# Two value tiles written to memory and read back row by row through indexed transfers

## The chip, the cores and the metric

The kernel runs on one core of a Trainium2 chip. The core has TensorE (PE in the profile; PEld is its weight load), VectorE (DVE), ScalarE (ACT), GpSimd (POOL) and SyncE (SP), which issues most of the transfers. Each engine works through its own list of instructions in order and waits on semaphores for the others. Transfers run on 16 DMA engines; SP and POOL each issue theirs on a queue of their own. The metric is the device time of one execution in microseconds (us), lower is better.

## The reference, cut to what matters

```python
# q, k, v: (4, 8, 768, 64); centroids: (8, 16, 64); w_in: (512, 2048); w_out: (2048, 512)
q_assign = argmax(q_n @ c_n.T); k_assign = argmax(k_n @ c_n.T)      # per head, 16 clusters
scores = q @ k.T / 8, masked to q_assign == k_assign
attn   = softmax(scores);  x = attn @ v                             # (4, 8, 768, 64)
x      = x.transpose(0, 2, 1, 3).reshape(3072, 512)
h = x @ w_in;  g = h - tanh(h);  out = g @ w_out                    # (3072, 512)
```

So there are 4 batches of 8 heads with 768 tokens each, an attention in which a token sees only the tokens of its own cluster, and a two-layer block on the result.

## The kernel before, in words

**Pairs and steps.** The eight heads of a batch are taken two at a time. A pair is `n` = 0 to 15: pairs 0 to 3 are the first batch, pairs 12 to 15 the fourth. The queries of a pair are cut into two halves of 384, its keys into six blocks of 128. A step is (pair, half, two key blocks), so a pair has six steps and there are 96 in all. In the late batches the steps follow each other pair by pair.

**What a step does.** One loop over the steps (`for at, (n, half, s) in enumerate(steps)`, L1223) writes the order of every engine by hand:

- `begin` (L491) issues the next step's scores on PE (`sc`, L499) and their exponential on ACT (L521).
- `value` (L549) multiplies the weights `e` by the values: `av` on PE, L556. It reads `vals[n][:, h, j]`, the 128 x 64 block of head `h` and key block `j`, and a step takes two of the six blocks, in order.
- `select` (L523) masks the next step's exponentials on DVE (`e`, L531), and after the second of a step's two tiles POOL adds the weights up into `sum` (L543 for the first step of a half, L547 twice for the others). The weights live in a pool of two buffers, so the mask of a step needs POOL's sum of the step two before to be done.
- After both halves of a pair, `total_both` (L610) adds `sum` over the partitions with four small matmuls on PE (`den`, L617). They wait for POOL's last addition to `sum`.

**What is put between.** While a batch's pairs run, the two-layer block of the batch before is put between the steps' matmuls (`fills`, L1214). From the first step of pair 12 it is the third batch's: first eight rounds `i` of seven products on PE (`pu`, L933), whose results DVE adds into `G` (L928); ACT takes the tanh of each round's two parts (`th`, L1000, a pool of two buffers), POOL subtracts it (`G`, L1002) and makes two further combinations per round (L1007, L1008). Then come 21 products `pd` (L1029) that read all of `G`. The first of them needs every round's first part.

**The queue of small jobs.** What else a step has to do is collected in the list `todo` (L1302), which is dealt out evenly between the products of the step (`between`, L1358). `turn`, `route_on` and `publish` of the next pair, the check of the weights' range (L1156) and the like are in it.

**The values.** A pair's values are loaded by SP with two transfers (L333, 192 KB each, one per head) into one of two buffers of `vals`, at the end of the pair two before. The load of pair 13 is issued by SP at 576.12 us, that of pair 14 at 632.22 us, that of pair 15 at 689.74 us. Nothing else touches `vals` before `value` reads it.

**POOL's transfers before.** POOL issues 32 loads of raw weights (L218) and 30 stores of results (L755, L1048); each moves 128 rows. The instruction waits for the transfer that used the same one of eight semaphores before it.

Of the kernel before, what the change touches and what calls it, by code (L numbers as in the profile page):

```python
# [30 lines left out]
F32 = mybir.dt.float32  # L31
BF16 = mybir.dt.bfloat16
I32 = mybir.dt.int32
# [6 lines left out]
P = 128  # L40
# [18 lines left out]
def kernel(  # L59
# [10 lines left out]
    nc = tc.nc  # L70
# [3 lines left out]
    B, H, S, D = q.shape  # L74
# [3 lines left out]
    NCH = S // P  # L78
    HP = H // 2
# [13 lines left out]
    const = ctx.enter_context(tc.tile_pool(name="const", bufs=1))  # L93
    dram = ctx.enter_context(tc.tile_pool(name="dram", bufs=6, space=DRAM))
# [84 lines left out]
    def fast():  # L179
# [48 lines left out]
            fetch(at + AHEAD)  # L228

        def constants():  # L230
            nc.vector.memset(inverses, 0.0)
            make_identity(nc, ident)
            nc.vector.memset(ones, 1.0 / words)
            nc.vector.memset(wholes, 0.0)

            mine_first = const.tile([P, 1], F32, name="mine_first")
            nc.vector.tensor_reduce(
                out=mine_first, in_=ident.rearrange("p (a b) -> p a b", b=D // 2)[:, :, 0], axis=AX.X,
                op=ALU.add,
            )  # L240
            nc.vector.tensor_copy(out=firsts, in_=mine_first.to_broadcast([P, D]))
            for c in range(C):
                nc.vector.memset(down[:, c : c + 1], float(C - c))

            spread_ = const.tile([P, 2, D], F32, name="spread_")
            nc.vector.memset(spread_, 0.0)
            nc.vector.tensor_copy(
                out=spread_[:, :, 0:C], in_=down.unsqueeze(1).to_broadcast([P, 2, C])
            )
            spread_ = spread_.rearrange("p a c -> p (a c)")  # L250
            nc.vector.tensor_tensor(out=spread_, in0=spread_, in1=ident, op=ALU.mult)
            nc.vector.reduce_sum(out=mine_code, in_=spread_, axis=AX.X)
# [54 lines left out]
        raw_qk, vals, turned, codes, q_codes = {}, {}, {}, {}, {}  # L307
# [5 lines left out]
        def rowwise(n: int):  # L313

            return n < HP

        def load(n: int, what=(0, 1)):
            if n >= len(pairs):
                return
            b, p = pairs[n]  # L320
            for i in what:
                if i < 2:
                    pool, tag = (gp, "g") if b == 0 else (loads, f"x{i}")
                    shape = [P, NCH, 2, D] if rowwise(n) else [P, NBL, BL]
                    t = raw_qk[n, i] = pool.tile(shape, F32, name=f"x{i}", tag=tag)
                else:
                    pool = vp0 if n in (2, 3) else vp
                    t = vals[n] = pool.tile([P, 2, NCH, D], F32, name="vals")
                for h in range(2):
                    src = (q, k, v)[i][b, 2 * p + h]  # L330
                    if i == 2 or rowwise(n):
                        order = "(p j) d -> p j d" if i and rowwise(n) else "(j p) d -> p j d"
                        nc.sync.dma_start(  # L333
                            t[:, :, h] if i < 2 else t[:, h], src.rearrange(order, p=P)
                        )
                        continue
                    blocks = src.rearrange("(b t) d -> t b d", t=BL)
                    for w in range(D // BL):
                        r = h * D + w * BL
                        nc.sync.dma_start(t[r : r + BL], blocks[:, :, w * BL : (w + 1) * BL])  # L340

        def turn(n: int, i: int, engine):

            if not rowwise(n):
                x = raw_qk.pop((n, i))
                pool = turnp0 if n in (2, 3) else turnp
                t = turned[n, i] = pool.tile([P, 2, TB], F32, name=f"t{i}")
                nc.vector.transpose(  # L348
                    out=t.rearrange("p a n -> p (a n)"), in_=x.rearrange("p b d -> p (b d)")
                )  # L350
                return
            pt = ps_s.tile([P, 2, 512], F32, name="pt", tag="s")
            x = raw_qk.pop((n, i))
            for j in range(NCH):
                nc.tensor.transpose(
                    out=pt[:, j // HCH, (j % HCH) * P : (j % HCH + 1) * P],
                    in_=x[:, j].rearrange("p h d -> p (h d)"), identity=ident,
                )
            pool = turnp0 if n in (2, 3) else turnp
            t = turned[n, i] = pool.tile([P, 2, TB], F32, name=f"t{i}")  # L360
            if engine is nc.scalar:
                nc.scalar.copy(out=t, in_=pt[:, :, 0:TB])
            else:
                nc.vector.tensor_copy(out=t, in_=pt[:, :, 0:TB])
# [75 lines left out]
        rows, hots = {}, {}  # L440
# [551 lines left out]
        def strassen_items(b: int):  # L992
# [82 lines left out]
        steps = [(p, half, s) for half in range(2) for p in range(HP) for s in range(NS)] + [  # L1075
            (n, half, s) for n in range(HP, len(pairs)) for half in range(2) for s in range(NS)
        ]
# [20 lines left out]


        ready = {}  # L1100
        TURN_Q, LOAD = 6, 7
        for n in range(2, len(pairs)):
            if n < HP:
                first_step, places = 3 * (n - 2), (0, 1, 1, 2, 2, 4)
            else:
                first_step = steps.index((n - 1, 0, 0) if n > HP else (n - 2, 1, 0))
                places = (-1, 0, 1, 3)
            for i, stage in enumerate(before(n)):
                if stage:
                    ready.setdefault(first_step + places[i], {})[i] = stage  # L1110
            if n >= HP:
                ready.setdefault(first_step + 1, {})[LOAD] = lambda n=n: load(n + 1)
                if not rowwise(n):
                    ready[first_step - 1][TURN_Q] = lambda n=n: turn(n, 0, nc.vector)
                ready[first_step + 1][2] = [
                    lambda n=n: similar(n), lambda n=n: turn_back(n), lambda n=n: route(n),
                    lambda n=n: route_on(n),
                ]
# [43 lines left out]
        rounding = list(range(len(PIECES)))  # L1162
        centroid_load()
        load(0)
        constants()
        keep_warm(7)
        centroid_norms()
# [3 lines left out]
        for i in range(AHEAD):  # L1171
            fetch(i)
        load(1)
        load(0, (2,))
        turn(0, 0, nc.scalar)
# [47 lines left out]
        for at, (n, half, s) in enumerate(steps):  # L1223
# [78 lines left out]
            todo = []  # L1302
# [4 lines left out]
                    todo.insert(len(todo) - 1, lambda n=n: total_both(n))  # L1307
            if LOAD in stages:
                stages[LOAD]()
            if TURN_Q in stages:  # L1310
                todo += [stages[0], stages[TURN_Q]]
            todo += [stages[i] for i in (5, 3, 4) if i in stages]
# [37 lines left out]
            if 2 * HALF <= at < 3 * HALF:  # L1350
# [3 lines left out]
                todo = todo[masks:]  # L1354
# [204 lines left out]
    with ExitStack() as cx, tc.manual_schedule():  # L1559
        fast()  # L1560
# [35 lines left out]
```

## Time and profile before

| | us |
|---|---|
| median of 2 runs (from, to) | 957.68 (957.45, 957.92) |
| the profiled execution, own time | 958.52 |
| its span in the profile | 956.7 |
| PE busy | 941.8 (98%) |
| DVE busy | 571.2 (60%) |
| POOL busy | 512.1 (54%) |
| ACT busy | 292.6 (31%) |

The clock granted to TensorE is 1.0 over the whole execution. The median, the profiled time and the span lie within 2 us of each other. "Busy" of POOL includes its arithmetic; the profile's page does not count the instructions that only issue transfers. A line of a timeline gives start, duration, engine, line of the kernel, operation, output and inputs with their shapes, how many equal instructions were merged, and in square brackets how long the engine had been idle before it and whom it waited for.

### The profile page before, as it was taken

To read this page: it belongs to the slowest core of one execution; us is meant where nothing else is said; L and a number is where in the kernel's file an instruction comes from. 1 tells how busy PE (TensorE), PEld (TensorE's weight loads), DVE (VectorE), ACT (ScalarE), POOL (GpSimd) and SP (SyncE) were. 2 spreads that over 40 slices of the span, in tenths; PEclk is the share of its full clock that TensorE was granted. 3 is DMA by queue.
4 is the path that set the end of the run, shared out by engine and by line. 5 is a ranking of instruction groups with operands and counts; after the bars stand their busy time and mean duration, and the time that the engine had idled before them with its cause. 6 is when DMAs were issued, how large, how long until landed. Compare 5 with 4: busy or idle time off the path is not lost.

```text
span 956.7 us, 16942 instructions
## 1 busy us (share of the span) xinstructions
PE 941.8 (98%) x6584; PEld 458.6 (48%) x6584; DVE 571.2 (60%) x1098; ACT 292.6 (31%) x453; POOL 512.1 (54%) x364
## 2 busy tenths in 40 slices
PE   8999999999999999999999999999999999999997
PEld 5433443345653333444455554444455555445664
DVE  7657676976776677666845567766754346443011
ACT  5575554223332332323321212333331220222000
POOL 1026353456775464777684453867796353657500
PEclk9999999999999999999999999999999999999999
DMA  7766455992736645474574746457334223323321
GB/s 196 200 188 147 141 153 128 261 258 88 196 117 157 158 143 122 151 175 130 189 191 148 181 146 184 111 179 173 110 125 146 98 81 103 116 78 132 107 106 36
DMA packets 166764, 139.85 MB, mean 146 GB/s; under 512 B 116580, under 2 KB 145044, under 8 KB 163988
## 3 DMA queue, kind: packets, MB, share of 16 engines
q1 hardware_dynamic: 160292, 117.15, 44.4%
q0 software_dynamic: 6240, 21.50, 6.8%
q8 instruction: 54, 0.88, 0.4%
q14 instruction: 34, 0.28, 0.1%
q10 hardware_dynamic: 144, 0.03, 0.0%
HBM read 117.48 MB, written 21.17 MB: 145 GB/s over the span
## 4 chain that ended last, share of the span: by engine, by line
PE 92%; DVE 2%; DMA 1%; ACT 1%; issue 1%; SPq 0%; DVEq 0%; ACTq 0%
PE pu L933 26%; PE pd L1029 23%; PE sc L499 14%; PE av L556 13%; PE o L746 8%; PE h L730 4%; PE sim L376 1%; DMA stream<-up_factors 1%; PE den L571 1%; PE den L617 1%; DVE e L531 1%; PE den L590 1%; DVE diff L899 0%; PE pq L432 0%; DVE t L348 0%
## 5 line engine op out<-in xcount | busy, mean ns | idle before, releaser
L547 POOL TENSOR_TENSOR sum<-sum,e 128x768 f32<-128x768 f32 x112 | 207.4, 1852 | 94.4 <-DVE e L531 90.2
L531 DVE SCALAR_TENSOR_TENSOR e<-row,code,sc 128x384 f32<-128x384 bf16 x336 | 185.9, 608 | 67.3 <-ACT sc L521 59.7
L521 ACT ACTIVATE sc<-sc 128x768 f32<-128x768 f32 x168 | 125.9, 789 | 229.5 <-PE sc L499 211.8
L1029 PE MATMUL pd<-stream,G 128*64 128x256 f32 x1728 | 191.2, 379 | 0.0
L933 PE MATMUL pu<-xT,stream 128*64 128x384 f32 (+1 forms) x1024 | 159.0, 447 | 1.7 <-DMA stream<-up_factors 1.1
L1029 PEld LDWEIGHTS pd<-stream,G 128*64 128x64 f32 x1728 | 123.9, 137 | 66.9 <-issue 7.2
L499 PE MATMUL sc<-t,t 64*128 64x384 f32 x768 | 150.2, 509 | 0.4 <-ACT e L521 0.3
L556 PE MATMUL av<-e,vals 128*64 128x384 f32 x768 | 145.9, 499 | 1.3 <-DVE e L531 1.3
L1002 POOL TENSOR_TENSOR G<-G,th 128x768 f32<-128x768 f32 (+1 forms) x51 | 87.1, 1724 | 69.4 <-ACT th L1000 69.2
L933 PE MATMUL pu<-diff,stream 128*64 128x384 f32 (+1 forms) x768 | 121.1, 448 | 2.8 <-DVE G L928 1.8
L933 PEld LDWEIGHTS pu<-xT,stream 128*64 128x64 f32 x1024 | 73.1, 137 | 75.8 <-issue 61.4
L499 PEld LDWEIGHTS sc<-t,t 64*128 64x128 f32 x768 | 65.9, 186 | 73.8 <-issue 37.6
L556 PEld LDWEIGHTS av<-e,vals 128*64 128x64 f32 x768 | 46.9, 136 | 86.3 <-issue 82.0
L1000 ACT ACTIVATE th<-G 128x768 f32<-128x768 f32 (+1 forms) x51 | 40.9, 806 | 148.9 <-DVE G L928 144.2
L543 POOL TENSOR_TENSOR sum<-e 128x768 f32<-128x768 f32 x28 | 52.6, 1879 | 62.8 <-DVE e L531 42.2
L746 PE MATMUL o<-w_out,g 128*64 128x512 f32 x384 | 86.1, 593 | 0.0
L933 PEld LDWEIGHTS pu<-diff,stream 128*64 128x64 f32 x768 | 53.8, 137 | 59.3 <-issue 45.2
L928 DVE TENSOR_TENSOR G<-pu,u 128x384 f32<-128x384 f32 x72 | 39.7, 552 | 32.9 <-PE pu L933 32.9
L1040 DVE SCALAR_TENSOR_TENSOR c<-pd,du 128x256 f32<-128x256 f32 x36 | 15.2, 421 | 67.1 <-PE pd L1029 67.1
L746 PEld LDWEIGHTS o<-w_out,g 128*64 128x64 f32 x384 | 27.4, 137 | 50.1 <-issue 50.0
L1040 DVE SCALAR_TENSOR_TENSOR du<-pd,du 128x256 f32<-128x256 f32 x27 | 11.4, 420 | 60.8 <-PE pd L1029 60.8
L730 PE MATMUL h<-xT,w_in 128*64 128x384 f32 x256 | 42.8, 486 | 0.0
(137 smaller groups left out, 827.0 us busy)
## 6 DMA issues: line engine op xcount, KB each, us to landing
stream<-up_factors SPq DMA_DIRECT2D x32, 896.0 KB
stream<-down_factors SPq DMA_DIRECT2D x21, 1024.0 KB
raw<-in_moe_w_in_dram POOLq DMA_DIRECT2D x16, 512.0 KB, 5.0
raw<-in_moe_w_out_dram POOLq DMA_DIRECT2D x16, 512.0 KB, 4.7
again<-in_moe_w_in_dram SPq DMA_DIRECT2D x32, 256.0 KB
again<-in_moe_w_out_dram SPq DMA_DIRECT2D x32, 256.0 KB
vals<-in_v_dram SPq DMA_DIRECT2D x32, 192.0 KB
row<-q_codes SPq DMA_DIRECT2D x29, 192.0 KB
```

The costliest lines, as they stand in the source:

```text
L499: nc.tensor.matmul(sc[i][:, h, 0:TB], lhsT=turned[n, 1][r].rearrange("p a n -> p (a n)")[:, j * P : (j + 1) * P], rhs=turned[n, 0][r, half ...
L521: nc.scalar.activation(out=out, in_=sc[i][:, :, 0:TB], func=ACT.Exp, scale=SCALE)
L531: nc.vector.scalar_tensor_tensor(out=e[:, h].rearrange("p (j n) -> p j n", n=P), in0=rows[n, half][:, h], scalar=(codes[n][:, h, 1, j : j ...
L543: nc.gpsimd.tensor_tensor(out=s, in0=pair[0], in1=pair[1], op=ALU.add)
L547: nc.gpsimd.tensor_tensor(out=s, in0=s, in1=pair[i], op=ALU.add)
L556: nc.tensor.matmul(avs[n, half][h * D : h * D + D], lhsT=vals[n][:, h, j], rhs=e[i][:, h], start=(j == 0), stop=(j == NCH - 1),)
L730: nc.tensor.matmul(h[r], lhsT=w_in[i][:, c, o * P : (o + 1) * P][:, r], rhs=xT[c][:, half], start=(c == 0), stop=(c == CD - 1),)
L746: nc.tensor.matmul(acc[sub][r], lhsT=gs[f % HF][:, f // HF, sub * P : (sub + 1) * P][:, r], rhs=w_out[f // FQ][:, f % FQ], start=(f == seq ...
L933: nc.tensor.matmul(ps[r], lhsT=streams[base + i][:, c, k_, r], rhs=right[c], start=(c == 0), stop=(c == CH - 1),)
L1000: nc.scalar.activation(out=th, in_=t, func=ACT.Tanh)
L1002: nc.gpsimd.tensor_tensor(out=t, in0=t, in1=th, op=ALU.subtract)
L1029: nc.tensor.matmul(ps[r], lhsT=left(i)[:, r], rhs=t[:, i], start=(i == 0), stop=(i == HF - 1))
```

## The change

Pairs 13 and 14 (`BY_ROWS`) get a detour for their values. When a pair's values have been loaded, twelve transfers per pair (six key blocks, two heads), issued by POOL, write them to a tile in memory of 768 rows of 64 numbers per head; twelve more read them back to the same place. Each of these 48 transfers has 128 rows of 256 B, and its rows' places in memory come from a column of indices on the chip, `places_of[:, j]`, which holds `j * 128 + p` for partition `p`: plain order. What is read back is what was written, to where it was.

The jobs are appended to `todo` in the steps of the pair before: with `at` the first step of pair `n - 1`, key blocks 0 to 2 are written in step `at + 1` and 3 to 5 in `at + 2`; blocks 0 to 2 are read back in `at + 3` and 3 to 5 in `at + 4`. A read waits for all six writes of its head. The index tile is made once at the start by POOL, ahead of the identity matrix.

```diff
         def constants():
+            nc.gpsimd.iota(places_of, pattern=[[P, NCH]], base=0, channel_multiplier=1, ...)
...
+        BY_ROWS = (3 * HP + 1, 3 * HP + 2)
+        places_of = const.tile([P, NCH], I32, name="places_of")
+        row_stores, row_moves = {}, {}
+
+        def rows_out(n: int, j: int):
+            for h in range(2):
+                if (n, h) not in row_stores:
+                    row_stores[n, h] = dram.tile([S, D], F32, name=f"rows_out{h}", bufs=len(BY_ROWS))
+                moved = nc.gpsimd.indirect_dma_start(
+                    row_stores[n, h], bass.IndirectOffsetOnAxis(ap=places_of[:, j : j + 1], axis=0),
+                    vals[n][:, h, j], None,
+                )
...
+        def rows_back(n: int, j: int):
+            for h in range(2):
+                moved = nc.gpsimd.indirect_dma_start(
+                    vals[n][:, h, j], None, row_stores[n, h],
+                    bass.IndirectOffsetOnAxis(ap=places_of[:, j : j + 1], axis=0),
+                )
+                for other_ in row_moves[n, h]:
+                    tc.add_manual_dep(moved.ins, other_.ins.name, ...)
...
+        moves = {}
+        for n in BY_ROWS:
+            for j in range(NCH):
+                at = steps.index((n - 1, 0, 0))
+                moves.setdefault(at + 1 + j // 3, []).append(lambda n=n, j=j: rows_out(n, j))
+                moves.setdefault(at + 3 + j // 3, []).append(lambda n=n, j=j: rows_back(n, j))
...
             if LOAD in stages:
                 stages[LOAD]()
+            todo += moves.pop(at, [])
             if TURN_Q in stages:
```

On POOL's list the 48 transfers fall into the stretch from 603 to 694 us of the profile before. With `W` for a write and `R` for a read, and lines of the kernel before for what stood there already, POOL's new order is:

```
pair 13: 6 W | L1002 x2, L1007, L1008, L543 | 6 W | L1002 x2, L1007, L1008, L547 x2 | 6 R | L1002,
         L547 x2 | 2 R | L1002 | 4 R | L1007, L1008, L543, L1002 x2, L1007, L1008, L547 x4, L1002
pair 14: 6 W | L1002, L1007, L1008, L543 | 6 W | L1002 x2, L1007, L1008, L547 x2 | 6 R | L547 x2,
         L1002 | 4 R | L1002 | 2 R | L1007, L1008, L1002, L543
```

On PE, DVE and SP no instruction is added; in the steps that got new jobs a few small ones (the transpose L432 and the copy L434 of the codes, the group L386 to L414, the mask L531, a check L1156, the store L438) move by about one product. `av` of pairs 13 and 14 (L556) now also waits for the reads.

More of the change, by code (lines that the diff above doesn't have):

```diff
@@ L230, in constants @@
         def constants():
+            nc.gpsimd.iota(
+                places_of, pattern=[[P, NCH]], base=0, channel_multiplier=1,
+                allow_small_or_imprecise_dtypes=True,
+            )
             nc.vector.memset(inverses, 0.0)
@@ L340, in load @@
                         nc.sync.dma_start(t[r : r + BL], blocks[:, :, w * BL : (w + 1) * BL])
+        BY_ROWS = (3 * HP + 1, 3 * HP + 2)
[9 more added lines that the diff above has]
+                )
+                for other_ in row_moves.setdefault((n, h), []):
+                    tc.declare_no_dep(moved.ins, other_.ins, reason="rows of one permutation")
+                row_moves[n, h].append(moved)
+        def rows_back(n: int, j: int):
[3 more added lines that the diff above has]
+                    bass.IndirectOffsetOnAxis(ap=places_of[:, j : j + 1], axis=0),
+                )
+                for other_ in row_moves[n, h]:
+                    tc.add_manual_dep(
+                        moved.ins, other_.ins.name,
+                        mybir.DependencyInfo(mybir.DependencyClass.Sync, mybir.DependencyReason.DATA),
+                    )
         def turn(n: int, i: int, engine):
```

## The prediction

> **What bounds the kernel now.** I read the busy times first, then the slices, then the stretch that the change touches.
>
> ```profile
> span 956.7 us, 16942 instructions
> ...
> PE 941.8 (98%) x6584; PEld 458.6 (48%) x6584; DVE 571.2 (60%) x1098; ACT 292.6 (31%) x453; POOL 512.1 (54%) x364
> ...
> POOL 1026353456775464777684453867796353657500
> ```
>
> PE is busy for 98% of the span, so nothing that PE loses can be made good later, and an instruction on another engine costs time only when PE ends up waiting for it. POOL's 54% is a mean: its slices 26 to 29 read 8, 6, 7, 7 and 9, 6 follow. The change puts all its instructions on POOL just there, so I asked for the busy times by stage:
>
> ```profile
> 603.00:700.00 97.00, 96.78 (x592) 40.73 (x590) 65.21 (x129) 34.21 (x51) 70.71 (x46) 1.00 0.51 150
> 700.00:800.00 100.00, 100.00 (x819) 57.48 (x817) 45.85 (x89) 19.95 (x31) 60.53 (x42) 1.00 0.32 107
> ```
>
> The columns are the stretch, its length, then busy time (and instructions) of PE, PEld, DVE, ACT, POOL, then clock, share of the DMA engines and GB/s. In the 97 us that take the 48 new transfers, POOL is busy for 70.7 and free for 26, and PE is full. The hundred microseconds after it are full on PE as well (100.00 of 100.00), so a delay of PE here goes to the end of the kernel undiminished. The DMA engines have half their time left.
>
> Where POOL's free time lies is shown by its timeline (rows left out in between are those where it ran on without a pause):
>
> ```profile
> 599.03 3.71 POOL L547 TENSOR_TENSOR sum<-sum,e 128x768 f32<-128x768 f32 x2 [5.68 <-DVE e L531]
> 604.58 3.60 POOL L1002 TENSOR_TENSOR G<-G,th 128x768 f32<-128x768 f32 x2 [1.84 <-ACT th L1000]
> ...
> 627.69 1.83 POOL L1002 TENSOR_TENSOR G<-G,th 128x768 f32<-128x768 f32 x1 [6.07 <-ACT th L1000]
> 629.48 3.70 POOL L547 TENSOR_TENSOR sum<-sum,e 128x768 f32<-128x768 f32 x2
> ...
> 641.26 3.60 POOL L1002 TENSOR_TENSOR G<-G,th 128x768 f32<-128x768 f32 x2 [2.36 <-ACT th L1000]
> ...
> 653.68 3.73 POOL L547 TENSOR_TENSOR sum<-sum,e 128x768 f32<-128x768 f32 x2 [3.00 <-DVE e L531]
> ...
> 665.95 1.82 POOL L543 TENSOR_TENSOR sum<-e 128x768 f32<-128x768 f32 x1 [2.84 <-DVE e L531]
> 668.59 3.59 POOL L1002 TENSOR_TENSOR G<-G,th 128x768 f32<-128x768 f32 x2 [0.82 <-ACT th L1000]
> ...
> 684.07 1.82 POOL L1002 TENSOR_TENSOR G<-G,th 128x768 f32<-128x768 f32 x1 [6.07 <-ACT th L1000]
> 685.85 4.23 POOL L547 TENSOR_TENSOR sum<-sum,e 128x768 f32<-128x768 f32 x2
> ...
> 693.97 1.00 POOL L1002 TENSOR_TENSOR G<-G,th 128x384 f32<-128x384 f32 x1
> ```
>
> The pauses from 602.74 (599.03 + 3.71) to 693.97 are 1.84 + 6.07 + 2.36 + 3.00 + 2.84 + 0.82 + 6.07 = 23.0 us. That is all that POOL has to give.
>
> Who notices when POOL is late? The chain of waits has these two among its rows (start, duration, what):
>
> ```profile
> 634.76 0.78 PE den L617 x8
> ...
> 689.85 1.12 PE den L617 x7
> ```
>
> `den` adds up POOL's `sum` at the end of pairs 12 and 13. PE takes its list in order, so at these two places it stands until POOL's L547 is done. The first comes 1.5 us after POOL's addition ends (629.48 + 3.70 = 633.18; PE's own row starts at 634.69); at the second the addition ends at 685.85 + 4.23 = 690.08 while `den` is already running: no reserve.
>
> **The change part by part.** *Removed*: nothing. *Added*: 48 transfers of 128 rows on POOL's list. The trace has no indexed transfer; its nearest rows are POOL's plain stores of 128 rows:
>
> ```profile
> L1048 POOL DMA_DIRECT2D out_dram<-c x24: 539/557/565, 495.7 to 806.3; - x24
> ...
> DMA to landing us min/median/max: 2.0/3.2/6.3
> ```
>
> The numbers are ns of one issue (least, median, most) and the time until the data has landed. Call the issue time of one indexed transfer x. From below, x is 0.56 us: as many rows, and nothing left out. From above I take 2.0 us, the shortest landing, as if the instruction held POOL until the data were there. Within that I take 1.30 us: an address per row must be formed from an index where a plain transfer steps on by a constant, so I count the 0.56 us twice (1.12), and add 0.18 us, the row of POOL's 128x1 copy into `gate` (L1170), for reading the column of indices. This is an estimate, and the whole answer hangs on it.
>
> Two rules of the Trainium skill pull it to opposite sides. "DMA: Bandwidth & Descriptors", section "Anatomy of one DMA — SWDGE (gpsimd) path", holds the making of descriptors to be small and says many can be made before it shows; by it x would stay near the plain row and the change would be free. "GPSIMD Engine Reference", section 7, prices small reads such as one per gather index at about 102 cycles each without overlap; at its 1.2 GHz, 128 of them would be about 10.9 us per transfer, an estimate from that page that would make the sum nearly 500 us. No row of this trace shows either.
>
> Now the sum, along POOL's new order.
>
> 1. *Up to the first `den`*: 12 writes and 6 reads stand ahead of L547 at 629.48. POOL falls behind by 18x; the pauses 1.84 and 6.07 and the 1.5 us of reserve are taken off. PE waits 18 × 1.30 − 9.4 = 14.0 us. On the way the tanh (L1000, two buffers) starts to wait for L1002 at about 627 (12 × 1.30 − 1.84 = 13.8 us late; 612.22 + 1.79 + 13.8 = 627.8 against 626.77), which is the same delay seen earlier, not another.
> 2. *From there to the second `den`*: POOL starts 1.5 us behind PE; 6 reads, 12 writes, 6 reads come, 24x = 31.2; the pauses 2.36, 3.00, 2.84, 0.82 and 6.07 (15.1) are taken off, and 1.8 for one L1002 that now stands behind the addition. PE waits 1.5 + 31.2 − 15.1 − 1.8 = 15.8 us.
> 3. *From there to the first `pd`*: 6 reads and that L1002 stand ahead of the L1002 at 693.97, 6x + 1.8 = 9.6. That row ends at 694.97; the first `pd` needs the last round's part only with its 15th of 16 matmuls, 14 × 0.216 us after its start at 699.04, so at 702: 7.0 us of reserve. PE waits 2.6 us.
>
> Together 14.0 + 15.8 + 2.6 = 32.4 us, or 48x − 30 wherever all three are positive. If x is 0.56, the first gives 0.7 and the others nothing.
>
> *The added waits.* The first write of a pair waits for the load of its values: SP issues pair 13's at 576.12 and pair 14's at 632.22, POOL comes to the writes at 602.7 and later than 660.9. The first read of a head waits for six writes, the last of which was issued before L1002 twice, L1007, L1008 and L547 twice: 3.6 + 1.0 + 1.0 + 3.7 = 9.3 us, against 6.3 us for the slowest landing. Were that cover gone, POOL would stand for the rest of a landing, with its sums queued behind. `av` waits for the reads: the last four of pair 13 are issued 6 × 1.30 + 1.8 = 9.6 us after the first `den`'s addition and land by 16 us, and PE needs them at 659.84, 26.7 us after it. For the others the margin is 6 us or more. All of it is free. *Memory traffic* is 48 × 32 KB twice over, 3 MB in some 90 us, with half the DMA time free: nothing.
>
> *Moved*: the small jobs on PE, DVE and SP go back or forth by about one product (1.29 us). The store of the codes (L438) goes behind one stream load; its reader L454 feeds a mask more than a step later, so the step covers it; without cover it would cost that 1.3 us, twice. *The index tile*: POOL makes it ahead of the identity. By the rows for the identity (0.20 and 0.29 us) it takes about 0.3 us; DVE first reads the identity at 1.67 us, it is ready at 1.31. Free, or some 0.3 us where not.
>
> Added to the profiled time, 958.5 + 32.4 = 990.9; the median stands 0.8 us lower, so I say 990.
>
> **The rivals.** *Cheap rows* (the other side): an indexed issue costs hardly more than a plain one, POOL's pauses swallow it, and the end stays. For it speaks that the plain rows need only 4 ns per row (0.53 to 0.57 us whether rows are 4 KB or 1 KB). Against it: POOL must fetch 128 indices first. Below x = 0.64 the sum is nothing; within 2% (19.2 us) it stays up to x = 1.02. At 0.56 it gives 958.4, at 0.8 about 966.
>
> *Dear rows*: x above 2 us, because the indices are read one at a time. At 2.5 us the sum is 48 × 2.5 − 30 = 90, that is 1048. Against it: POOL's arithmetic takes 128x768 numbers in 1.8 us, so 128 of something should not take longer unless each is fetched alone.
>
> *The transfers, not POOL*: reads land late and PE waits in `av` rather than in `den`. If every landing took the longest 6.3 us, the margins above still hold; with cheap rows the fourth read of pair 14 is issued 2 × 0.56 + 3.7 = 4.8 us before the addition for `den` ends and needed at 696.41, 6.3 us after it, so a landing of 15 us would cost PE 3.9 us, 962. *Not what it says*: the rows come back unchanged in any case; if they did not move at all it would be 957.7, and the order of instructions speaks against it.
>
> **How the numbers follow.** A measurement of this kernel tells about 2% from no change. Forecast (x from 1.02 to 2.0): 0.55. Cheap rows, with the small rivals: 0.35, of which 0.02 for a gain over 2%, since nothing is removed. Dear rows: 0.10. The range takes both bounds of x, 0.56 us (959) and 2.0 us (48 × 2.0 − 30 = 66, 1024), and leaves out the dear rows. Faster 0.02, same 0.33, slower 0.65.
>
> **What would show it.** Right: POOL's slices from 603 to 720 near 9, 48 issue rows on POOL of about 1.3 us, waits of `den` L617 and tanh L1000 for POOL of some 14 and 16 us, pauses of POOL gone, PE's products later by 32 us and otherwise equal. Step 1 is wrong if PE waits in `av` or in the mask (`e` L531) rather than at the first `den`. The forecast falls if the issue rows are under 1 us (cheap) or above 2 us (dear), or if VectorE and POOL slow each other down in the crowded stretch, which I have not priced.

## The result, and the profile after

| us | before | after |
|---|---|---|
| median (from, to), 2 runs each | 957.68 (957.45, 957.92) | 989.37 (988.44, 990.29) |
| the profiled execution, own time | 958.52 | 990.29 |
| its span | 956.7 | 988.4 |
| PE busy | 941.8 | 947.0 |
| POOL busy | 512.1 | 557.9 |

The ratio is 1.0331, 95% interval 1.0286 to 1.0375: slower by 31.7 us. In two later series, on two different chips, the changed kernel stood at 987.85 (985.82 to 988.73) and 986.90 us (986.26 to 988.23), ratios 1.0309 (1.0292 to 1.0326) and 1.0311 (1.0294 to 1.0328), which is some 30 us. Line numbers from here on are those of the changed kernel: the writes are L355, the reads L366, `den` L651, `sum` L577 and L581, `pu` L967, `pd` L1063, the tanh L1034, and POOL's combinations of `G` L1036, L1041 and L1042.

First the page of the changed kernel: span, busy times, and the slices of PE, POOL and the granted clock.

```profile
span 988.4 us, 17008 instructions
...
PE 947.0 (96%) x6584; PEld 459.6 (46%) x6584; DVE 569.9 (58%) x1098; ACT 292.7 (30%) x453; POOL 557.9 (56%) x413
...
PE   8999999999999999999999999779689999999997
...
POOL 1025443557655657677964356899899445466600
PEclk9999999999999999999999999979989999999999
```

POOL gained 45.8 us of work and its mean moved by two points of per cent. The slices tell more: slices 26 to 31 of POOL, counted from 1 and 24.7 us long each, read 8, 9, 9, 8, 9, 9, and it is there that PE falls to 7, 7, 9, 6 and 8. PE's number of matmuls is unchanged. Two slices of the clock read 7 and 8 where before there was nothing but 9.

The rows of the new instructions (duration in ns, least, median, most; then how long POOL paused before them, and the time to landing):

```profile
L355 POOL DMA_INDIRECT rows_out<-vals,places_of x24: 963/968/1049, 604.6 to 697.3; - x24
...
  issue: 6.6, 23
...
DMA to landing us min/median/max: 2.1/3.5/8.0
...
L366 POOL DMA_INDIRECT vals<-rows_out,places_of x24: 948/952/989, 636.7 to 729.2; - x24
```

One issue is 0.95 to 0.97 us, and ahead of nearly each lie about 0.30 us (6.6 / 23) in which POOL does nothing and waits for nobody. Together a write holds POOL for 1.27 us and a read for 1.25. No row of the profile has an engine waiting for `rows_out` or for the reads into `vals`.

Who waits? The list of waits between 590 and 745 us (total, times, longest), and PE's timeline at the two `den`:

```profile
ACT th L1034 <- POOL G L1036: 32.8, 7, 17.9
...
PE den L651 <- POOL sum L581: 24.0, 2, 12.3
```

```profile
649.54 1.50 PE L651 MATMUL den<-sum,ones 128*32 128x384 f32 x4 [12.31 <-POOL sum L581]
650.96 4.15 PE L967 MATMUL pu<-diff,stream 128*64 128x384 f32 x16
654.94 1.46 PE L967 MATMUL pu<-xT,stream 128*64 128x384 f32 x8
...
719.29 1.50 PE L651 MATMUL den<-sum,ones 128*32 128x384 f32 x4 [11.71 <-POOL sum L581]
```

PE is idle for 24.0 us at the second halves of the two `den`, and waits elsewhere in these 155 us for 0.4 us only. The 24 products after the first wait are slow at first: the x16 take 4.15 us. The stretches show why (length, then busy time of PE, PEld, DVE, ACT, POOL, then clock, share of the DMA engines, GB/s):

```profile
637.00:649.50 12.50, 0.23 (x2) 0.00 (x0) 2.27 (x5) 0.00 (x0) 10.86 (x9) 0.62 0.22 80
649.50:656.40 6.90, 6.86 (x30) 2.31 (x30) 2.56 (x4) 0.49 (x1) 5.69 (x6) 0.69 0.05 15
656.40:707.00 50.60, 50.23 (x307) 21.44 (x309) 32.53 (x67) 16.11 (x23) 46.03 (x36) 1.00 0.58 155
707.00:719.30 12.30, 0.59 (x6) 0.01 (x2) 0.41 (x1) 0.00 (x0) 10.53 (x10) 0.69 0.42 131
719.30:727.10 7.80, 7.80 (x30) 2.58 (x30) 4.65 (x8) 2.71 (x5) 6.73 (x6) 0.61 0.05 18
```

For some 7 us after each wait PE works at a mean granted clock of 0.69 and 0.61. The chain of waits has the 24 products as one row each time; before, both took 4.02 us:

```profile
651.03 5.37 PE pu L967 x24
...
720.79 6.32 PE pu L967 x24
```

With the starts of these rows the 31.7 us between the two spans can be placed. The rows of the kernel before, and the first `pd` after:

```profile
635.55 4.02 PE pu L933 x24
690.97 4.02 PE pu L933 x24
699.21 6.91 PE pd L1029 x64
```

```profile
731.33 6.91 PE pd L1063 x64
```

1.7 us were lost ahead of the stretch already (POOL's L581 before the first write starts at 600.72 instead of 599.03). They are this execution's and not the change's: in the two later profiles of the changed kernel the same row starts at 598.84 and 599.31 us. Up to the `pu` after the first `den`: 651.03 − 635.55 − 1.7 = 13.8 us. From there to the `pu` after the second: 720.79 − 690.97 − 15.5 = 14.3 us. From there to the first `pd`: 731.33 − 699.21 − 29.8 = 2.3 us. After that 0.4 us come back.

### The profile page after: what moved, and what is told of

It is laid out like the page before. It is cut to its first block, busy times and chain, and to the rows that moved or that the text cites. A ratio compares the mean times of both kernels' runs of the same rounds, so it can differ in the third digit from the quotient of the medians.

```text
span 988.4 us, 17008 instructions
## 1 busy us (share of the span) xinstructions
PE 947.0 (96%) x6584; PEld 459.6 (46%) x6584; DVE 569.9 (58%) x1098; ACT 292.7 (30%) x453; POOL 557.9 (56%) x413
## 4 chain that ended last, share of the span: by engine, by line
PE 80%; POOL 8%; DVE 5%; DMA 3%; issue 3%; ACT 1%; SPq 0%; POOLq 0%; DVEq 0%; ACTq 0%
PE pd L1063 22%; PE pu L967 20%; PE sc L533 11%; PE av L590 11%; PE o L780 6%; PE h L764 4%; POOL rows_out L355 2%; POOL sum L581 2%; POOL G L1036 2%; DVE e L565 1%; PE sim L410 1%; DMA hot<-q_codes 1%; POOL vals L366 1%; PE den L651 1%; DMA stream<-up_factors 1%
## 5 line engine op out<-in xcount | busy, mean ns | idle before, releaser
L581 POOL TENSOR_TENSOR sum<-sum,e 128x768 f32<-128x768 f32 x112 | 207.0, 1848 | 92.5 <-DVE e L565 88.2
L1063 PE MATMUL pd<-stream,G 128*64 128x256 f32 x1728 | 191.2, 379 | 0.0
L967 PE MATMUL pu<-xT,stream 128*64 128x384 f32 (+1 forms) x1024 | 160.5, 450 | 1.9 <-DMA stream<-up_factors 1.2
L1063 PEld LDWEIGHTS pd<-stream,G 128*64 128x64 f32 x1728 | 123.9, 137 | 66.9 <-issue 7.2
L967 PE MATMUL pu<-diff,stream 128*64 128x384 f32 (+1 forms) x768 | 123.3, 455 | 2.8 <-DVE G L962 1.8
L1036 POOL TENSOR_TENSOR G<-G,th 128x768 f32<-128x768 f32 (+1 forms) x51 | 87.2, 1727 | 50.3 <-ACT th L1034 50.1
L967 PEld LDWEIGHTS pu<-xT,stream 128*64 128x64 f32 x1024 | 73.3, 137 | 76.6 <-issue 62.2
L1034 ACT ACTIVATE th<-G 128x768 f32<-128x768 f32 (+1 forms) x51 | 40.8, 805 | 170.7 <-DVE G L962 133.2
L577 POOL TENSOR_TENSOR sum<-e 128x768 f32<-128x768 f32 x28 | 52.7, 1881 | 59.5 <-DVE e L565 38.9
L967 PEld LDWEIGHTS pu<-diff,stream 128*64 128x64 f32 x768 | 54.9, 139 | 62.5 <-issue 48.9
L1074 DVE SCALAR_TENSOR_TENSOR c<-pd,du 128x256 f32<-128x256 f32 x36 | 15.1, 421 | 67.2 <-PE pd L1063 67.2
```

Source lines behind the costliest of these rows:

```text
L577: nc.gpsimd.tensor_tensor(out=s, in0=pair[0], in1=pair[1], op=ALU.add)
L581: nc.gpsimd.tensor_tensor(out=s, in0=s, in1=pair[i], op=ALU.add)
L967: nc.tensor.matmul(ps[r], lhsT=streams[base + i][:, c, k_, r], rhs=right[c], start=(c == 0), stop=(c == CH - 1),)
L1034: nc.scalar.activation(out=th, in_=t, func=ACT.Tanh)
L1036: nc.gpsimd.tensor_tensor(out=t, in0=t, in1=th, op=ALU.subtract)
L1063: nc.tensor.matmul(ps[r], lhsT=left(i)[:, r], rhs=t[:, i], start=(i == 0), stop=(i == HF - 1))
```

## The experiments

The theory was: POOL's fixed cost of an indexed issue, times 48, fills POOL between 603 and 730 us, and PE waits at `den`. The rivals: the detour through memory itself (traffic, landings, the added waits); a cost that goes by rows or by bytes; the two places of `den` rather than POOL's whole list; and a slow TensorE as a cost of its own. Unless it says otherwise the number is a median with the range of its runs, and the ratio is to the kernel before on the same chip.

### The same 48 transfers without indices (e1_plain_pool, e2_plain_sp)

```diff
-                moved = nc.gpsimd.indirect_dma_start(
-                    row_stores[n, h], bass.IndirectOffsetOnAxis(ap=places_of[:, j : j + 1], axis=0),
-                    vals[n][:, h, j], None,
-                )
+                moved = nc.gpsimd.dma_start(row_stores[n, h][j * P : (j + 1) * P], vals[n][:, h, j])
```

The read is changed likewise; rows, places, order and waits stay. In the second kernel SP issues them (`nc.sync` in place of `nc.gpsimd`).

> The same 48 transfers at the same places of POOL's list, with the same waits and bytes, but plain: the rows' places are written into the instruction instead of being read from the index tile. Theory (POOL's time for making an indexed transfer is what costs): an issue takes about 0.58 us as POOL's plain stores do, 18 x 0.58 - 9.4 = 1 us of waiting at the first den and nothing after, so 957 to 961 us. Rival (the traffic, its landing or the added waits cost): those are unchanged, so 985 to 991 us, with PE waiting in av or at den as in the changed kernel.

> The same 48 plain transfers, issued by SP instead of POOL. Theory: POOL's list is as before the change, no wait of PE for POOL at den beyond the one of before, 956 to 960 us. Rival (the detour through memory and the waits of av for it): 985 to 991 us. If SP's own list is delayed by them, PE would wait for the streams instead, 960 to 970 us.

Measured: 957.33 us (956.35 to 958.64), ratio 0.9992 (0.9980 to 1.0005), and 957.33 us (956.33 to 958.55), ratio 0.9990 (0.9979 to 1.0001). The rows of the writes, and POOL's timeline, in the kernel where POOL issues them:

```profile
L355 POOL DMA_DIRECT2D rows_out<-vals x24: 537/537/568, 601.9 to 670.0; - x24
```

```profile
601.88 3.20 POOL L355 DMA_DIRECT2D rows_out<-vals  x6
```

Six plain issues take 3.20 us, 0.53 us each and nothing between them, against 6 × 1.27 = 7.6 us. PE waits at neither `den`. So the traffic, the landings, the added waits, the moved small jobs and the index tile, which is still made here, cost nothing; all 30 us hang on the indexed form of the instruction. In this kernel, which makes the index tile too, the L575 ahead of the first write starts at 598.22 us, earlier than the 599.03 us of the kernel before.

### Half the rows in each (e3_half_rows)

```diff
-                places_of, pattern=[[P, NCH]], base=0, channel_multiplier=1,
+                places_of, pattern=[[D, NCH]], base=0, channel_multiplier=1,
...
-                    row_stores[n, h], bass.IndirectOffsetOnAxis(ap=places_of[:, j : j + 1], axis=0),
-                    vals[n][:, h, j], None,
+                    row_stores[n, h], bass.IndirectOffsetOnAxis(ap=places_of[0:D, j : j + 1], axis=0),
+                    vals[n][0:D, h, j], None,
```

Only the first 64 of the 128 rows of each block make the detour, the others stay where they are.

> The 48 indexed transfers move only the first 64 of 128 rows each (the other half of the values stays in place). Theory: the time follows 48x - 30 with the x that its own issue rows show (gap included). If x is per row, 1.27 becomes about 0.65 us and the time is 957 to 962 us; if most of x is fixed per instruction (above 0.95 us), 971 to 986 us. Rival (bytes): half the delay, 973 us, whatever x is.

Measured: 984.87 us (984.19 to 985.96), ratio 1.0271 (1.0244 to 1.0298). The rows of the writes, and PE at the two `den`:

```profile
L355 POOL DMA_INDIRECT rows_out<-vals,places_of x24: 897/902/972, 603.0 to 693.4; - x24
```

```profile
646.73 1.50 PE L651 MATMUL den<-sum,ones 128*32 128x384 f32 x4 [9.88 <-POOL sum L581]
...
714.97 1.50 PE L651 MATMUL den<-sum,ones 128*32 128x384 f32 x4 [8.63 <-POOL sum L581]
```

With half the rows the issue is shorter by 0.07 us, 1 ns per row; the pause of 0.30 us is unchanged. x is 1.20, and 48 × 1.20 − 30 = 27.6 us against 27.0 measured. The cost is one of the instruction, not of its rows, and my reason for the size of x was wrong.

### Half the transfers, each twice as wide (e4_wide_rows)

```diff
-                    vals[n][:, h, j], None,
+                    vals[n][:, h, 2 * j : 2 * j + 2].rearrange("p a d -> p (a d)"), None,
...
-            for j in range(NCH):
+            for j in range(NCH // 2):
```

24 indexed transfers of 128 rows of 512 B: the same bytes, half the instructions. The places of the jobs are set to match (`j // 2`).

> Two key blocks per indexed transfer: rows of 512 B instead of 256 B, 24 transfers of 128 rows instead of 48, the same bytes. Theory: x stays near 1.27 us as the number of rows per transfer does; ahead of the first den stand 10 transfers (10 x 1.27 - 9.4 = 3.3 us), of the second 12 more (12 x 1.27 less the pauses, about 1 us), so 960 to 965 us. Rival (bytes, or time per byte): 985 to 991 us, with x near 2.5 us.

Measured: 964.14 us (963.36 to 965.21), ratio 1.0061 (1.0043 to 1.0079). The rows of the writes, and PE's timeline:

```profile
L355 POOL DMA_INDIRECT rows_out<-vals,places_of x12: 963/976/1048, 602.5 to 675.7; - x12
```

```profile
637.32 1.48 PE L651 MATMUL den<-sum,ones 128*32 128x384 f32 x4 [2.17 <-POOL sum L581]
638.74 3.80 PE L967 MATMUL pu<-diff,stream 128*64 128x384 f32 x16
...
696.92 0.84 PE L651 MATMUL den<-sum,ones 128*32 128x384 f32 x4 [2.04 <-POOL sum L581]
697.69 1.51 PE L967 MATMUL pu<-xT,stream 128*64 128x384 f32 x8
```

An issue of 64 KB holds POOL as long as one of 32 KB. Half the instructions take away nearly 24 of the 30 us: 24 × 1.27 = 30.5 us of issuing stand against 23.0 us of pauses. The two waits are alike, 2.17 and 2.04 us, but only after the first are the products slow (3.80 us for 16, and 1.48 for the half of `den`, where 2.8 and 0.84 are usual).

### The changed kernel again (e5_changed_again, e10_changed_third)

Run unchanged as the yardstick of the next four.

> The changed kernel as it stands, as the yardstick for the three others on this chip. Both theories: 988 to 991 us, granted clock below 0.75 in the 7 to 8 us after each of the two waits of TensorE at `den` (L651, some 12 us each), and the 24 products `pu` that follow take about 5.4 and 6.3 us where they took 4.02 us before.

> The changed kernel as it stands, beside e9_repeated on the same chip: 987 to 990 us by both theories; `pu` x24 takes 5 us or more after each of the two waits at `den`.

Measured: 987.85 and 986.90 us, as told above. PE idles 12.20 and 9.75 us at the two `den` in the first, 12.28 and 11.42 us in the second; the 24 `pu` after the two `den` of the first run take 4.99 and 5.84 us (5.4 and 6.3 were expected), and in the second the x16 among those after the first `den` take 4.41 us where 2.80 are usual. Both medians lie 0.1 to 0.2 us under what was expected. The granted clock in the 7 to 8 us after the waits was 0.75 and 0.67, then 0.66 and 0.79. In e5_changed_again PE also waited 2.2 us for `G` at two `pu` ahead of the second `den`.

### The two `den` put off by one step (e7_den_later)

```diff
-                    todo.insert(len(todo) - 1, lambda n=n: total_both(n))
+                    if n in (3 * HP, 3 * HP + 1):
+                        put_off.append(lambda n=n: total_both(n))
+                    else:
+                        todo.insert(len(todo) - 1, lambda n=n: total_both(n))
```

`put_off` is dealt out with the next step's jobs, what follows `den` is put off with it, and one more buffer holds `sum` meanwhile. The 48 transfers are unchanged.

> The small products `den` of pairs 12 and 13 and what follows them are put off by one step (some 9 to 10 us), so that POOL has that much more time for the sum they read; one more buffer for `sum`. All 48 indexed transfers stay. Theory (POOL's list is longer than the stretch, and `den` is only the first place where it shows): the waits at `den` shrink from 12 us to 0 to 5 us, but PE then stands for POOL further on (masks held up by POOL's sums, tanh held up by L1036, at the latest `pd`); total 980 to 990 us. Rival (the two places of `den` are the price, an order with more room there costs little): 962 to 970 us.

Measured: 988.33 us (986.83 to 990.52), ratio 1.0321 (1.0302 to 1.0341), no better than the 987.85 of the changed kernel beside it. PE's waits from 600 to 740 us (total, times, longest):

```profile
PE sc L533 <- DVE e L565: 6.7, 1, 6.7
PE den L651 <- POOL sum L581: 3.7, 1, 3.7
PE pu L967 <- ACT s L972: 3.2, 1, 3.2
PE pd L1063 <- POOL G L1036: 2.5, 1, 2.5
PE pq L466 <- ACT s L972: 1.9, 1, 1.9
PE pu L967 <- DVE G L962: 1.4, 1, 1.4
```

The wait at `den` fell from 22.0 us to 3.7, and the time did not move. PE now waits in five other places: for a mask, twice for ACT, whose tanh waits 39.0 us for POOL's L1036 in this kernel, for `G`, and at `pd`. This speaks clearly against the rival: `den` is where POOL's lateness shows first; with the wait there taken away, the same time is lost behind it.

### All transfers one step earlier (e8_one_step_earlier)

```diff
-                moves.setdefault(at + 1 + j // 3, []).append(lambda n=n, j=j: rows_out(n, j))
-                moves.setdefault(at + 3 + j // 3, []).append(lambda n=n, j=j: rows_back(n, j))
+                moves.setdefault(at + 0 + j // 3, []).append(lambda n=n, j=j: rows_out(n, j))
+                moves.setdefault(at + 2 + j // 3, []).append(lambda n=n, j=j: rows_back(n, j))
```

> All 48 indexed transfers are put one step earlier (writes in steps 0 and 1 of the pair before, reads in steps 2 and 3). POOL gains the pause of 5.68 us that lies ahead of the stretch now. Theory (at each `den` the issue times of all transfers ahead of it, less the pauses, are waited for): all 24 transfers of a pair now stand ahead of its `den`: 24 x 1.27 - 5.7 - 9.4 = 15.4 us at the first, some 16 us less the reserve at the second, nothing left for `pd`; with 2 to 6 us for slow products after the waits, 986 to 993 us: no better, though fewer transfers are in the end in the way of `pd`. Rival (only the pauses in the whole stretch count, and one more of 5.7 us is used): 982 to 985 us.

Measured: 993.86 us (992.52 to 997.52), ratio 1.0374 (1.0357 to 1.0392), 6 us above the changed kernel and 0.9 us above the theory's range, in which two of the four runs lie. The profile is of the slowest of the four, 997.52 us. The rival, a gain of some 5 us, falls. At the first `den` the sum held: the `pu` behind it starts at 653.83, against 635.55 before, and 2.8 us of that lie ahead of the stretch in this run, so 15.5 us against 15.4 expected. At the second it was 18.8 us against some 16. Between the two, POOL stood for 2.57 us and waited for the tanh, which was late itself:

```profile
660.54 3.60 POOL L1036 TENSOR_TENSOR G<-G,th 128x768 f32<-128x768 f32 x2 [2.57 <-ACT th L1034]
```

The last L1036 ended at 731.40 us, 9.4 us before `pd` needed it (737.74 + 14 × 0.216): what POOL had left there was of no use any more, since PE had lost its time at the two `den`. To have all 24 transfers of a pair ahead of its `den` costs more than the pause of 5.7 us gives.

### TensorE kept busy while it waits (e6_filled, e9_repeated, e11_repeated_more)

Do the slow products cost anything, and what makes them slow? In e6_filled matmuls that nobody reads stand between the two halves of `den`:

```diff
+        WARM = 44
+        def fill_pe(times: int):
+            warm = ps_a.tile([P, TB], F32, name="warm_late", tag="a")
+            for _ in range(times):
+                nc.tensor.matmul(
...
+                if half == 1 and n in (3 * HP, 3 * HP + 1):
+                    fill_pe(WARM)
```

> 44 matmuls of 128x256 whose result nobody reads are put on TensorE between the first and the second half of `den` of pairs 12 and 13 (about 0.24 us each, some 10.7 us), so that TensorE works where it stood idle. The output is unchanged. Theory (the slow products after the wait come from TensorE having been idle): the clock stays at 1.0, `pu` x24 takes 4.0 us both times; the first place gains about 2.4 us of PE time, which is given back in part as a longer wait at the second `den`, since POOL is what is late; the 2.3 us lost before `pd` turn into a wait for POOL's L1036. Total 986 to 990 us. Rival (the products are slow because the stretch is crowded, whatever TensorE did before): they still take 5.4 and 6.3 us and the total stays at 989 to 991 us with the clock low.

Measured: 1014.74 us (1013.53 to 1016.54), ratio 1.0598 (1.0580 to 1.0616): the filling was mis-sized, 19.3 us in the first place, and in the second it waited 13.8 us for a buffer of its own. The total says nothing on the question, but the first place does. PE's timeline there:

```profile
635.91 19.26 PE L617 MATMUL warm_late<-bd,ident 128*128 128x256 f32 x88
655.10 0.84 PE L663 MATMUL den<-sum,ones 128*32 128x384 f32 x4
655.87 2.80 PE L979 MATMUL pu<-diff,stream 128*64 128x384 f32 x16
658.50 1.46 PE L979 MATMUL pu<-xT,stream 128*64 128x384 f32 x8
```

PE did not pause, and `pu` ran at full speed (4.02 us for the 24), with POOL as full as in the changed kernel. In the second place, with 13.8 us of idling up to 725.65, the clock was 0.50 from 719.3 to 727.1 us and 0.83 in the 7.9 us after.

The next two repeat the first half of `den` instead, 14 times, and then 18 and 20 times:

```diff
-                for h in range(2):
+                again = {3 * HP: 18, 3 * HP + 1: 20}.get(n, 1) if half == 0 else 1
+                for h in list(range(2)) * again:
```

> The filling of e6_filled was twice too long (88 passes of 0.22 us, 19.3 us, longer than the wait of 12.3 us), and in the second place it waited itself for a buffer. Here TensorE repeats what it has just done: the two products of the first half of `den` of pairs 12 and 13 are made 14 times instead of once (26 products more, about 0.385 us each, some 10 us), into the same place, with the same result. Theory (the slow products come from TensorE having been idle): 2 to 4 us of waiting are left at each `den`, the clock in the 7 us after it is 0.95 to 1.0, `pu` x24 takes 4.0 to 4.3 us both times; the 2.4 us so gained after the first `den` come back as waiting at the second, since POOL's list is as long as ever, and those before `pd` turn into a wait of about 2 us for POOL's L1036; total 985 to 988.5 us, 0 to 2.5 us below the changed kernel in the same series. Rival (the stretch is crowded): `pu` x24 still takes 5.4 and 6.3 us, total 988 to 992 us.

> As e9_repeated, with the two products of the first half of `den` made 18 times for pair 12 and 20 times for pair 13 (0.165 us per pass and two passes a product in e9_repeated, 9.22 us for 56 passes: 11.9 and 13.2 us), so that less than 2 us of waiting is left at each. Theory (gaps of TensorE of more than some 2 us bring its clock down; POOL's list sets the end of the stretch all the same): clock 0.97 to 1.0 after both, `pu` x24 takes 4.0 to 4.3 us, at least one of the two times; the time so gained comes back as a wait of the first `pd` (L1064) for POOL's L1037, 1.5 to 4 us where e9_repeated had 0.2; total 985 to 988.5 us, no gain on the changed kernel. Rival (the slow products are what a crowded POOL or the late values do to TensorE): they stay above 5 us and `pd` doesn't wait.

Measured: 987.43 us (986.60 to 988.58), ratio 1.0321 (1.0304 to 1.0338), beside 986.90 for the changed kernel; and 987.34 us (986.89 to 988.37), ratio 1.0304 (1.0283 to 1.0325). With 14 repeats, PE:

```profile
646.72 1.49 PE L652 MATMUL den<-sum,ones 128*32 128x384 f32 x4 [3.89 <-POOL sum L581]
648.14 4.82 PE L968 MATMUL pu<-diff,stream 128*64 128x384 f32 x16
```

Here I missed: waits of 3.89 and 2.73 us were left, as expected, but they sufficed to make the next products slow: the 24 took 6.04 us after the first wait, and after the second the x16 among them 2.96 us and the x8 2.83, where 2.75 and 1.51 are usual. `pd` waited 0.20 us for POOL where I had expected about 2. With 18 and 20 repeats:

```profile
634.00 11.80 PE L652 MATMUL den<-sum,ones 128*32 128x384 f32 x72
647.17 0.84 PE L652 MATMUL den<-sum,ones 128*32 128x384 f32 x4 [1.37 <-POOL sum L581]
647.94 2.80 PE L968 MATMUL pu<-diff,stream 128*64 128x384 f32 x16
...
731.00 4.11 PE L1064 MATMUL pd<-stream,G 128*64 128x256 f32 x36 [0.69 <-POOL G L1037]
```

```profile
PEclk9999999999999999999999999999999999999999
```

The clock stays at 1.00 in every stretch, the 24 `pu` take 4.02 us, and the total is what it was. So the slow clock comes from PE's idling, and it costs next to nothing here: what PE loses by it, it would else have spent waiting for POOL. In the first profile of the changed kernel `pd` comes to its 15th matmul 1.2 us after POOL's row had ended (731.33 + 14 × 0.216 against 733.19), so up to 1.2 us can be laid to the slow products; in e10_changed_third `pd` waits 0.29 us for that row, and they cost nothing. The wait at `pd` that I expected to grow to 1.5 us or more was 0.69; the filling of the second place was too long by about 1 us, and `pu` waited 1.4 us for `G` and 0.9 us for ACT on the way.

## Why the prediction was right, point by point

The forecast was 990 us, and 989.37 came.

**x = 1.30: right in size, wrong in its reason.** Measured 1.25 to 1.27. I had doubled the plain row because "an address per row must be formed from an index". But 64 rows instead of 128 save 0.07 us only, and wider rows cost nothing more. What there is in fact: 0.95 to 0.97 us of which some 0.84 are fixed (0.968 − 128 × 1.03 ns, by the difference of the two sizes), and a pause of 0.30 us before nearly each, for which I had no term at all. That the sum came out near was luck to that extent; the bounds of 0.56 and 2.0 us were the honest part. By the letter of my own sign, issue rows under 1 us, the forecast should have fallen: the rows are 0.95 to 0.97, and only the pause brings x over 1. With x = 1.27 the sum 48x − 30 is 31.0 us, with 1.25 it is 30.0, and the medians give 31.7, 30.0 and 29.9.

Two rules of the Trainium skill had been set against each other. "DMA: Bandwidth & Descriptors", section "Anatomy of one DMA — SWDGE (gpsimd) path", calls the making of descriptors small: per row that agrees with the 1 ns here, but the 0.84 + 0.30 us per instruction are what decided. "GPSIMD Engine Reference", section 7, with about 102 cycles per index (10.9 us per transfer, an estimate from that page) does not describe these transfers: 0.97 us was measured.

**Step 1, 14.0 us at the first `den`: 13.8 measured**, at that place and for that releaser. 12.31 us of it are idle time; the other 1.5 us are `den` itself, which was one row of 0.89 us for both halves where nothing is waited for, and is 0.84 + 1.50 us when its second half comes alone and slowly.

**Step 2, 15.8 us at the second: 14.3 measured.** With x = 1.27 the step's own sum is 1.5 + 30.5 − 15.1 − 1.8 = 15.1; the rest is in POOL's favour. It is made up otherwise than I thought: 11.71 us of idle time, and the rest is `den` split in two again and PE's slow products after the first wait (5.37 − 4.02 = 1.35 us), which I had not priced. They delayed PE, not POOL, so the idle time at the second `den` is that much shorter.

**Step 3, 2.6 us at the first `pd` for L1036: 2.3 measured, but in another form.** In the changed kernel's profile `pd` waits for nobody; the 2.3 us are the slow `pu` (6.32 − 4.02) after the second `den`. The wait that I forecast stands right behind: where PE lost less it appears, at the 15th of the 16 matmuls as worked out, 2.5 us in e7_den_later and 0.69 us in e11_repeated_more. So the price was right to within 1.2 us because both end at the same row of POOL.

**One sum over POOL.** The same total comes from POOL alone. From the L581 ahead of the first write to the end of the last round's first part (L1036) it needs 694.97 − 599.03 = 95.94 us before and 733.19 − 600.72 = 132.47 us after, 36.5 us more, without one pause over 0.31 us. The two rows of the changed kernel:

```profile
600.72 3.72 POOL L581 TENSOR_TENSOR sum<-sum,e 128x768 f32<-128x768 f32 x2 [5.68 <-DVE e L565]
...
732.18 1.01 POOL L1036 TENSOR_TENSOR G<-G,th 128x384 f32<-128x384 f32 x1
```

Less the 7.0 us of reserve at `pd`, PE must be late by 29.5 us, wherever it waits. In the profiles of e5, e7, e9, e10 and e11 the same stretch takes 132.1 to 132.7 us. e7_den_later moved the waits, e11_repeated_more took the slow clock away, and neither moved the total: that is what this sum says. VectorE and POOL slowing each other, which I had not priced, does not show: POOL's L1036 x2 take 3.59 to 3.62 us where L1002 x2 took 3.58 to 3.60.

**What was costed at nothing** (the index tile, memory traffic, landings, the added waits, the moved small jobs) cost nothing: e1_plain_pool and e2_plain_sp have all of it and stand at 957.33 us. The longest landing was 8.0 us, beyond the 6.3 from which I had worked, and still inside the margin.

**The rivals.** *Cheap rows* needed x under 1.02, 0.25 us below what was measured; had the pause of 0.30 us not been there, x would have been 0.97 and the kernel within 2%. So the 0.35 that I gave it was not too much. My sentence that below x = 0.64 the sum is nothing was wrong: there only the second and third steps are nothing, and the first still gives 18 × 0.64 − 9.4 = 2.1 us. *Dear rows* had no case: no issue in the profiles of the changed kernel took over 1.05 us. Nor had *the transfers, not POOL*: nothing waits for the reads in the first profile, and one weight load for 0.2 us in e10_changed_third.

## What to carry to other kernels

Go along the list of the engine that got the new instructions, from one place to the next where the bounding engine needs something of it. At each, add up the time that the new instructions ahead of it hold the engine, subtract its pauses and the reserve there: the rest is waited for, and a bounding engine without free time does not make it up later. One sum over the whole stretch gives the same only where no pause or reserve on the way is left over, as in the changed kernel. By that one sum e8_one_step_earlier should have been 5.7 us faster than the changed kernel, and it was 6 us slower; e4_wide_rows should have been 24 × 1.27 − 30 = 0.5 us slower than the kernel before, and it was 6.2. Count an indexed transfer on POOL by instructions, not by rows or bytes: half as many, twice as wide, cut the loss from 30 to 6 us, and a plain transfer in known order cost nothing at all. A cost found in the profile (here slow products) must be taken away once before it is called a loss; this one was nearly free.

## What the runs showed of the hardware

- **An indexed issue on POOL** takes 0.97 us (write) or 0.95 us (read) at 128 rows, 0.90 us at 64 rows, and the same with 512 B per row as with 256 (0.976 and 0.968 us). Ahead of it lie about 0.30 us of nothing where another indexed issue comes before it and 0.15 to 0.17 us where arithmetic does; arithmetic follows it without a pause (611.08 + 0.97 us, then L1036 at 612.07). A plain one of the same data takes 0.54 us with no pause.
- **TensorE's clock after a pause.** After 10 to 12 us of idle time the mean granted clock was 0.61 to 0.79 over the next 7 to 8 us, in the three profiles of the changed kernel. Far shorter pauses did it as well: 3.89, 2.73 and 2.17 us each slowed the products after them, while 2.04 us (e4_wide_rows) and 1.37 us (e11_repeated_more) did not. After the 2.17 us in e4_wide_rows the second half of `den` took 1.48 us instead of 0.84, and 16 `pu` took 3.80 us instead of 2.80. In e8_one_step_earlier two pauses of 0.87 and 1.38 us, with a product of 0.28 us between them, were followed by 8 `pu` in 2.83 us instead of 1.51; with 0.19 and 1.38 us in e11_repeated_more they took 1.51.
- The Trainium skill, "TensorE: Matmul & The Clock Gate", Part 1, has the clock fall to half after an idle window of about 3.4 us that runs freely. The half fits the granted clock of 0.50 in e6_filled; but the pause of 2.17 us, shorter than that window, was enough here, and the one of 2.04 us was not. Where the border lies between runs stays open.
